# Moving the load buffer of a streaming decode kernel to a 256-byte boundary

## The chip, the cores and the metric

The kernel runs on one core of one Trainium2 chip. The metric is the device time of one execution in microseconds (us). Before the change it is 2518.53 us, the median of three runs.

## What is computed

One decode step of a layer that mixes attention with a gated MLP. The cache of keys and values is read once and used once, 32 heads of 65,536 positions of 128 numbers in bf16, so 1.07 GB of cache go through the core for a single output row of 512 numbers.

```python
def _A_ref(x, k_cache, v_cache, wq, wo):          # H=32, Sk=65536, Dh=128, Sq=1
    q = (x @ wq).reshape(B, Sq, H, Dh).transpose(0, 2, 1, 3)
    scores = einsum("bhqd,bhkd->bhqk", q, k_cache) * (Dh ** -0.5)
    o = einsum("bhqk,bhkd->bhqd", softmax(scores), v_cache)
    return o.transpose(0, 2, 1, 3).reshape(B, Sq, H * Dh) @ wo

def _B_ref(x, w_gate, w_up, w_down):              # D=512, F=1792
    return (silu(x @ w_gate) * (x @ w_up)) @ w_down

g = sigmoid((x * gate_w).sum(-1))
out = g * a + (1 - g) * b                         # a: attention, b: MLP
```

## The kernel before

One SBUF tensor, `mem` (L84), is 184 KB in each of the 128 partitions and takes every load from DRAM: the weights, the small vectors x and gate_w, all of K and V, and the output weights. Slots in it are counted in units of 1 KB (`KB = 512` bf16 numbers), and `at(kb, n)` (L109) gives the slice that starts at slot `kb`. K's halves go to slots 32 and 0, V's to 120 and 96 (`place`, L201), and weights use the same slots before and after K and V do.

A head is worked on in two halves (z = 0, 1) of 32,768 positions. One load brings one half of K or V of a head, 8 MB: each partition receives one contiguous row of 64 KB. Loads of that size are issued by SyncE from one queue (L224), in the order K half, V half, K half, V half, where V runs one head behind K. The loop over heads (L241 to L249) holds each load back until its slot is free: a K load waits until VectorE has transposed the half that lies there (`ktdone`), a V load until TensorE has multiplied it (`pvdone`).

VectorE turns K in pieces of 32 rows with 32x32 block transposes from `mem` into the small double buffer `kt` (L322, L415, L422). TensorE multiplies the pieces by the query (L472) into a bank of PSUM that holds a head's 65,536 scores as 128 x 512. VectorE and TensorE find the maximum (L336 to L338, L547, L549), ScalarE takes the exponential (L288), VectorE reorders the result into `pb` (L331), and TensorE multiplies it with V straight out of `mem`, 128 matmuls of 512 columns a head (L525). The order on each engine is written out by hand and held together by semaphores.

The start loads wq, w_gate, w_up and w_down (L213) and the first K half in two pieces (L228), and computes the query and the MLP. The end replaces the last V load by eight smaller ones with rows of 32 KB down to 1 KB (`tail`, L61 and L258), so that little work is left behind the last landing, and adds the output projection.

`sb` (L66) allocates an SBUF tensor with the allocator's default alignment. `mem` is the first tensor allocated in SBUF, and everything from `kt` on lies behind it.

Of the kernel before, what the change touches and what calls it, by code (L numbers as in the profile page):

```python
# [5 lines left out]
P = 128  # L6
KB = 512
# [5 lines left out]
BF16 = mybir.dt.bfloat16  # L13
# [8 lines left out]
def bass_gated_mix__mha_block_cached__swiglu_ffn__decode_kernel(  # L22
# [27 lines left out]
    MEM = 184  # L50
# [12 lines left out]
    WOJ, WO31 = V0, V0 + 1  # L63

    with ExitStack() as ctx:
        def sb(name, shape, dt):  # L66
            return ctx.enter_context(nc.sbuf_tensor(name, shape, dt))

        def psum(name, shape, dt):
            return ctx.enter_context(nc.psum_tensor(name, shape, dt))  # L70
# [10 lines left out]
        psW = psum("psW", [P, 512], F32)  # L81
        psZ = psum("psZ", [P, 512], F32)

        mem = sb("mem", [P, MEM * KB], BF16)  # L84
        kt = sb("kt", [P, 2, 2 * PR * 32], U32)
        qd = sb("qd", [P, H, 4, 4], BF16)
        qcur = sb("qcur", [P, 4, 4], BF16)
        pa = sb("pa", [P, 512], BF16)
# [542 lines left out]
```

## Time and profile before

| what | value |
|---|---|
| runs (median, lowest, highest) | 2518.53, 2518.48, 2519.13 us |
| span of the profiled execution, first to last instruction | 2517.0 us |
| busy: TensorE matmul, VectorE, ScalarE | 68%, 56%, 3% |
| bytes read from HBM, mean rate over the span | 1087.77 MB, 432 GB/s |
| mean granted TensorE clock | 0.721 |

The time of the profiled execution is its span, 2517.0 us; the median of the runs lies 1.5 us above it. In the profile, PE is TensorE, DVE is VectorE, ACT is ScalarE, SPq is SyncE's queue that issues DMAs, and L525 is line 525 of the kernel. A DMA is cut into packets, which the core's 16 DMA engines take. "Share of 16 engines" is the sum of the packets' durations over 16 times the length of the stretch that is looked at, so in a stretch shorter than a packet it can exceed 100%: a packet counts whole in the stretch in which it starts.

### The profile page before, as it was taken

The page shows a single profiled execution, that of the slowest core. Times are in us where ns is not written, and L with a number is a line of the kernel's source. Part 1 is how long each engine was busy: PE and PEld are TensorE (multiplying, and loading weights), DVE is VectorE, ACT ScalarE, POOL GpSimd, SP SyncE. Part 2 cuts the span into 40 slices and gives each one's busy share as a digit, 9 for nine tenths or more (in the row PEclk, how much of TensorE's full clock was granted, in tenths as well). Part 3 has the DMA queues.
Part 4 walks back from the last instruction along what each step waited for, and adds up shares of the span by engine and source line. Part 5 has one row for each costly group of instructions (what it writes and reads, how often), then busy time and mean ns, then how long its engine had stood idle before and what let it go on. Part 6 is the DMA issues. An engine that isn't in the chain of part 4 may idle for free.

```text
span 2517.0 us, 51694 instructions
## 1 busy us (share of the span) xinstructions
PE 1710.9 (68%) x21624; PEld 979.2 (39%) x21624; DVE 1411.7 (56%) x1683; ACT 64.6 (3%) x195; POOL 0.2 (0%) x4
## 2 busy tenths in 40 slices
PE   4667756667667677676776766766767767667677
PEld 3334433333433334333443333343334433334334
DVE  4764565554655645646456555465564564645653
ACT  0000000000000000000000000000000000000000
POOL 0000000000000000000000000000000000000000
PEclk8577767677677676776776767767767767677677
DMA  9999999999999999999999999999999999999999
GB/s 419 435 433 433 433 433 433 433 434 433 434 433 433 433 433 433 433 433 433 433 433 433 433 433 434 435 433 434 434 433 433 434 434 433 433 433 433 434 433 395
DMA packets 20471, 1087.93 MB, mean 432 GB/s; under 512 B 2283, under 2 KB 2669, under 8 KB 2925
## 3 DMA queue, kind: packets, MB, share of 16 engines
q1 hardware_dynamic: 20452, 1087.78, 99.9%
q8 instruction: 9, 0.15, 0.0%
q14 instruction: 2, 0.01, 0.0%
q10 hardware_dynamic: 8, 0.00, 0.0%
HBM read 1087.77 MB, written 0.00 MB: 432 GB/s over the span
## 4 chain that ended last, share of the span: by engine, by line
DMA 71%; PE 27%; DVE 1%; issue 1%; SPq 0%; ACT 0%; DVEq 0%
DMA mem<-in_A_v_cache_dram 68%; PE psO L525 27%; DMA mem<-in_A_k_cache_dram 2%; DVE kt L322 1%; DMA mem<-in_A_wq_dram 0%; DVE kt L415 0%; SPq L224 0%; PE psM L456 0%; DVE pb L331 0%; PE psS L472 0%; SPq L258 0%; PE psZ L600 0%; DVE sm L336 0%; PE psW L561 0%; PE psM L547 0%
## 5 line engine op out<-in xcount | busy, mean ns | idle before, releaser
L472 PE MATMUL psS<-qcur,kt 128*128 128x4 bf16 x16384 | 573.0, 169 | 728.7 <-DVE kt L415 413.2
L525 PE MATMUL psO<-mem,pb 128*4 128x512 bf16 x3968 | 1042.3, 429 | 34.5 <-DMA mem<-in_A_v_cache_dram 34.1
L472 PEld LDWEIGHTS psS<-qcur,kt 128*128 128x128 bf16 x16384 | 534.0, 105 | 792.1 <-issue 789.7
L422 DVE STREAM_TRANSPOSE kt<-mem 128x2048 uint32<-128x2048 uint32 x248 | 547.6, 2275 | 405.9 <-DMA mem<-in_A_k_cache_dram 405.9
L415 DVE STREAM_TRANSPOSE kt<-mem 128x2048 uint32<-128x2048 uint32 x248 | 551.3, 2280 | 239.3 <-DMA mem<-in_A_k_cache_dram 238.3
L525 PEld LDWEIGHTS psO<-mem,pb 128*4 128x4 bf16 x3968 | 359.8, 93 | 660.4 <-issue 241.3
L331 DVE COPY pb<-pa 32x64 bf16<-32x64 bf16 x1024 | 233.5, 228 | 15.1 <-ACT pa L288 1.5
L338 DVE TENSOR_REDUCE sc<-psM 1x1 f32<-1x128 f32 x32 | 8.9, 279 | 334.9 <-PE psM L547 334.9
L336 DVE TENSOR_REDUCE sm<-psS 128x1 f32<-128x512 f32 x32 | 22.1, 692 | 42.2 <-PE psS L472 42.2
L322 DVE STREAM_TRANSPOSE kt<-mem 128x2048 uint32<-128x2048 uint32 x16 | 35.4, 2277 | 16.9 <-DMA mem<-in_A_k_cache_dram 16.9
L286 ACT ACTIVATE sm<-psM 128x1 f32<-128x1 f32 x32 | 5.5, 171 | 1223.4 <-PE psM L549 1223.4
L282 ACT ACTIVATE oTn<-psT,gcol 128x1 f32 (+1 forms) x31 | 8.2, 264 | 1036.8 <-PE psT L499 1036.8
L499 PE MATMUL psT<-ident,orow 4*128 4x1 f32 x256 | 33.5, 248 | 0.5 <-ACT orow L280 0.5
L499 PEld LDWEIGHTS psT<-ident,orow 4*128 4x128 f32 x256 | 30.8, 186 | 1.2 <-ACT orow L280 0.6
L280 ACT ACTIVATE orow<-psO,sm 4x512 f32<-4x512 f32 x31 | 21.0, 678 | 130.3 <-PE psO L525 126.0
L288 ACT ACTIVATE pa<-psS,sm 128x512 bf16<-128x512 f32 x32 | 22.0, 687 | 1.0
L549 PE MATMUL psM<-sc,onesf 1*128 1x1 f32 x64 | 12.3, 259 | 11.9 <-DVE sc L338 11.9
L561 PE MATMUL psW<-pb,mem 128*128 128x1 bf16 x512 | 14.6, 165 | 6.5 <-DMA mem<-in_A_v_cache_dram 6.0
L549 PEld LDWEIGHTS psM<-sc,onesf 1*128 1x128 f32 x64 | 9.6, 186 | 21.5 <-DVE sc L338 21.5
L561 PEld LDWEIGHTS psW<-pb,mem 128*128 128x128 bf16 x512 | 14.1, 102 | 7.6 <-issue 5.5
L553 PEld LDWEIGHTS psM<-sm,onesf 128*128 128x128 f32 x64 | 9.7, 191 | 14.7 <-issue 13.5
L553 PE MATMUL psM<-sm,onesf 128*128 128x1 f32 x64 | 12.4, 264 | 1.1 <-ACT pa L288 1.1
(72 smaller groups left out, 93.1 us busy)
## 6 DMA issues: line engine op xcount, KB each, us to landing
mem<-in_A_v_cache_dram SPq DMA_DIRECT2D x3, 4096.0 KB, 29.4
mem<-in_A_k_cache_dram SPq DMA_DIRECT2D x2, 4096.0 KB, 38.9
mem<-in_A_wq_dram SPq DMA_DIRECT2D x1, 4096.0 KB, 12.3
mem<-in_A_wo_dram SPq DMA_DIRECT2D x1, 3968.0 KB, 36.6
mem<-in_A_v_cache_dram SPq DMA_DIRECT2D x1, 2048.0 KB, 32.9
mem<-in_B_w_gate_dram SPq DMA_DIRECT2D x1, 1792.0 KB, 16.1
mem<-in_B_w_up_dram SPq DMA_DIRECT2D x1, 1792.0 KB, 21.4
mem<-in_B_w_down_dram SPq DMA_DIRECT2D x1, 1792.0 KB, 25.2
```

The costliest lines, as they stand in the source:

```text
L288: nc.scalar.activation(pa[:], psS[:], ACT.Exp, bias=nbias, scale=SCALE, accum_out=rsum).then_inc(expdone, 1)
L322: nc.vector.transpose(kt[:, i % 2, :].rearrange("p (j r t) -> p r j t", j=2, t=32), src.rearrange("p (r j t) -> p r j t", j=2, t=32)).then ...
L331: last = nc.vector.tensor_copy(dst, sr)
L336: nc.vector.reduce_max(mxs, psS[:], AX_X).then_inc(s_mx, 1)
L415: nc.vector.transpose(kt[:, c % 2, :].rearrange("p (j r t) -> p r j t", j=2, t=32), src.rearrange("p (r j t) -> p r j t", j=2, t=32)).then ...
L422: nc.vector.transpose(kt[:, c % 2, :].rearrange("p (j r t) -> p r j t", j=2, t=32), src.rearrange("p (r j t) -> p r j t", j=2, t=32)).then ...
L472: last = nc.tensor.matmul(psS[:, o:o + 4] if j is None else psS[:, ds(j * (2 * PR) + o, 4)], ktb[b][:, je // 2, r, :, je % 2], qcur[:, je, ...
L499: last = nc.tensor.matmul(psT[:, 0:1], orow[0:4, i * Dh:(i + 1) * Dh], ident[0:4, i:i + 1], start=(i == 0), stop=(i == 3))
L525: last = nc.tensor.matmul(psO[0:4, :], pb[:, k_col[256 * z + r]:k_col[256 * z + r] + 4], vt[:, r * Dh:(r + 4) * Dh], start=(z == 0 and par ...
L549: nc.tensor.matmul(amx, onesf[0:1, :], gm, start=True, stop=True).then_inc(s_ar, 1)
L553: nc.tensor.matmul(Lt, onesf[:], rsum, start=True, stop=True).then_inc(s_L, 1)
L561: last = nc.tensor.matmul(psW[:, 0:1], vt[:, r * Dh:(r + 1) * Dh], pb[:, col:col + 1], start=(r0 + r == 0), stop=(r0 + r == R - 1))
```

## The change

`sb` gets an argument for the alignment, 32 bytes unless given, and `mem` is allocated with 256. In each partition `mem` then begins at byte 16640, which is 65 x 256, in place of byte 16512, which is 128 past 64 x 256. All slots of `mem` and every tensor behind it move up by 128 bytes. Nothing else changes: the instructions, their order, their waits and the DRAM sides of the loads are the same.

```diff
-        def sb(name, shape, dt):
-            return ctx.enter_context(nc.sbuf_tensor(name, shape, dt))
+        def sb(name, shape, dt, align=32):
+            return ctx.enter_context(nc.sbuf_tensor(name, shape, dt, align_bytes=align))
...
-        mem = sb("mem", [P, MEM * KB], BF16)
+        mem = sb("mem", [P, MEM * KB], BF16, 256)
```

## The prediction

> **What bounds the kernel now.** I read the page first for what is busy, then the chain of waits for what the end hangs on, then the DMA queue's own waits for how early each load is issued, and last the DMA packets in short stretches for what one packet costs.
>
> ```profile
> span 2517.0 us, 51694 instructions
> PE 1710.9 (68%) x21624; PEld 979.2 (39%) x21624; DVE 1411.7 (56%) x1683; ACT 64.6 (3%) x195; POOL 0.2 (0%) x4
> DMA  9999999999999999999999999999999999999999
> GB/s 419 435 433 433 433 433 433 433 434 433 434 433 433 433 433 433 433 433 433 433 433 433 433 433 434 435 433 434 434 433 433 434 434 433 433 433 433 434 433 395
> DMA packets 20471, 1087.93 MB, mean 432 GB/s; under 512 B 2283, under 2 KB 2669, under 8 KB 2925
> q1 hardware_dynamic: 20452, 1087.78, 99.9%
> DMA 71%; PE 27%; DVE 1%; issue 1%; SPq 0%; ACT 0%; DVEq 0%
> ```
>
> The DMA engines are busy in every slice, at 433 GB/s from the third slice to the next to last, while TensorE and VectorE are idle for a third and for nearly half of the span. The chain gives 27% to PE, which looks like a second limit. It is not one, and three pieces of the chain show why:
>
> ```profile
> 143.60 10.69 PE psO L525 x40
> ...
> 1006.82 26.85 DMA mem<-in_A_v_cache_dram
> 1033.71 11.07 PE psO L525 x40
> ...
> 2465.67 10.19 PE psO L525 x40
> ```
>
> From the first of these PE pieces to the last there are 60 steps, each of one 8 MB load of K and one of V. That is (2465.67 - 143.60) / 60 = 38.701 us a step, and 19.351 us a load. The load issued at 1006.82 lands 26.85 us later: it spends 7.5 us behind the load ahead of it and 19.35 us moving. The chain follows the issue through PE because a V buffer comes free only when PE has read it, but the queue never runs dry. What sets the time is therefore how fast the 16 engines swallow packets. Per packet the trace says this (one pitch of a load; then short stretches with one kind of packet in them):
>
> ```profile
> DMA packets 144, 8.39 MB, mean 434 GB/s; under 512 B 16, under 2 KB 16, under 8 KB 16
> ...
> q1 hardware_dynamic: 144, 8.39, 100.2%
> ```
>
> This is the stretch 985.00 to 1004.35 us. Each engine handles 9 packets: 8 rows of 64 KB and a completion packet under 512 B. Their durations add up to 1.002 x 19,350 = 19,389 ns, 38 more than the pitch of 19,351, so a packet overlaps its neighbour by about 4.2 ns. I take that off every duration below.
>
> ```profile
> DMA packets 2, 0.00 MB, mean 1 GB/s; under 512 B 2, under 2 KB 2, under 8 KB 2
> ...
> q1 hardware_dynamic: 2, 0.00, 11.2%
> ```
>
> ```profile
> DMA packets 14, 0.01 MB, mean 239 GB/s; under 512 B 0, under 2 KB 14, under 8 KB 14
> ...
> q1 hardware_dynamic: 14, 0.01, 67.1%
> ```
>
> ```profile
> DMA packets 7, 0.10 MB, mean 502 GB/s; under 512 B 0, under 2 KB 0, under 8 KB 0
> ...
> q1 hardware_dynamic: 7, 0.10, 117.0%
> ```
>
> The first is 315.51 to 315.52 us, two completion packets: 0.112 x 160 / 2 = 9.0 ns each. The second is 2513.42 to 2513.48, fourteen 1 KB rows: 0.671 x 960 / 14 = 46.0 ns. The third is 14.10 to 14.30, seven 14 KB rows (14,336 B) of the MLP weights: 1.170 x 3200 / 7 = 534.9 ns. From the second to the third are 13,312 B and 488.9 ns, so an engine moves 27.23 B per ns once a row runs. A 1 KB row is then 37.6 ns of bytes. Its 46.0 less the overlap of 4.2 is 41.8, so it pays **4.2 ns beyond its bytes**. A 64 KB row is (19,389 - 9) / 8 = 2422.5 ns, less 4.2, which is 2418.3; its bytes are 2406.8, so it pays 11.5 beyond them. That last figure is soft: one ns in the 488.9 shifts it by 5. A completion packet pays 9.0 - 4.2 - 0.1 = 4.7 ns beyond its few bytes.
>
> **The change part by part.** It removes and adds no instruction. It moves the base of mem from 128 past a multiple of 256 bytes to such a multiple. Every slot of mem is a multiple of 1 KB, so every row of every load moves from the middle of a 256-byte block to its start. Everything allocated after mem moves up by 128 bytes.
>
> *The rows.* All packets but those under 512 B are rows, and nearly all of them are in q1, the queue of the loads into mem: (20,471 - 2,283) / 16 = 1137 rows on each engine. Since the engines are busy to the end, a ns saved on a row is 1137 ns off the span. No row of the trace starts on a boundary, so the saving is not shown and I bound it. Below: a row may pay nothing for its start, and then nothing is saved. Above: the whole surplus may come from the start, 11.5 ns on each of the 64 KB rows, of which there are
>
> ```profile
> mem<-in_A_k_cache_dram SPq DMA_DIRECT2D x63, 29.5
> mem<-in_A_v_cache_dram SPq DMA_DIRECT2D x62, 27.5
> ```
>
> 125 x 8 = 1000 on an engine, and 4.2 ns on the other 137: 11.5 + 0.6 = 12.1 us. Below nothing I treat as a rival. Between the ends I take the time of half a block: a row that starts in the middle of a block has to touch one block more than its bytes fill, and the unused half is 128 / 27.23 = 4.7 ns. The nearest row is the 1 KB row with its 4.2 ns, short of that by half a ns. The sum is 1137 x 4.7 = 5.3 us.
>
> The Trainium skill bears on this in "DMA: Bandwidth & Descriptors", section "How a descriptor splits into AXI transactions": a transaction has to start at a 256-byte boundary, and a descriptor that does not start there pays beats for the unused bytes in front. It says so of reading, and mem is the written side here; the 4.2 ns of the trace agree in size, but show no start on a boundary to set against them. By its figures half a block is 4 beats at 850 MHz, an estimate of 4.7 ns, which would make the same sum.
>
> *The engines that read mem.* TensorE's reads in the value matmuls and VectorE's transposes get a new base too:
>
> ```profile
> L525 PE MATMUL psO<-mem,pb 128*4 128x512 bf16 x3968 | 1042.3, 429 | 34.5 <-DMA mem<-in_A_v_cache_dram 34.1
> L422 DVE STREAM_TRANSPOSE kt<-mem 128x2048 uint32<-128x2048 uint32 x248 | 547.6, 2275 | 405.9 <-DMA mem<-in_A_k_cache_dram 405.9
> L415 DVE STREAM_TRANSPOSE kt<-mem 128x2048 uint32<-128x2048 uint32 x248 | 551.3, 2280 | 239.3 <-DMA mem<-in_A_k_cache_dram 238.3
> ```
>
> I cost these at nothing, either way. VectorE waits 644 us for K, and a V load waits 7.5 us behind another, so PE would have to become 7.5 us slower in a step, on about 17 us of value matmuls (1042.3 / 62), before the queue ran dry. A gain there would go into the same waits. With that cover gone, each us a step would cost 60 us.
>
> *The faster queue.* At 2 x 8 x 4.7 ns the step shrinks by 0.075 us, and the wait behind the other load by a like amount out of 7.5. What is late next is still the DMA queue.
>
> *The end.* From the last row on nothing changes: the final matmuls, the copy and the store hang on the last landing, which comes earlier by the whole sum.
>
> The sum against the profiled execution is 2517.0 - 5.3 = 2511.7 us of span. The median of the runs, 2518.53, lies 1.5 above that span, so the forecast is 2518.5 - 5.3 = **2513.2 us**.
>
> **The rivals.**
>
> *A. A fixed price of any packet: no change.* The completion packet writes no row of mem and yet pays 4.7 ns, about what the 1 KB row pays. If that is the price of starting any packet, it stays, and the time is 2518.5 us. For it: the equal sums, from the same trace. Against it: a completion is another kind of write, with a start of its own that the trace does not show, so the two 4 to 5 ns need not have one cause. The skill's same page, section "Why small descriptors are slow (HBM only)", has a rule that speaks against the change in this way: about 3 cycles on each packet whatever its start. An estimate at the page's 850 MHz is 3.5 ns of the 4.2, which would leave 0.7 ns a row, under 1 us in all. No run here tells the two rules apart. That the base does not move as stated comes out as this rival too.
>
> *B. The whole surplus goes.* If being off the boundary also makes the long rows stumble (a row that sits astride each block all the way), all of the 11.5 ns goes: 2518.5 - 12.1 = 2506.4 us. For it: a 64 KB row pays more than a 1 KB row. Against it: the figure is soft, and 64 KB rows land while the engines read mem, which the 14 KB rows hardly do.
>
> *C. Slower: writes fall into step with the engines' reads.* A 64 KB row pays 11.5 - 4.2 = 7.3 ns more than a short one. If that comes from meeting the reads of L525, L415 and L422, and a row on a boundary meets them more often, because the reads then start on the same boundary, a doubling adds 7.3 ns to each of 1000 rows: 2518.5 + 7.3 = 2525.8 us. It decides from 5.0 ns a row on, where the loss passes 0.2%. Against it: the rate in the page's slices is the same 433 or 434 nearly everywhere, and writes and reads that met by chance would make it wander.
>
> **How the numbers follow.** About 0.2%, here 5.0 us, is what a measurement of this kernel can tell from no change; the three runs shown lie within 0.65 us. The forecast's 5.3 us is barely past that, and 4.2 ns a row instead of 4.7 would be 4.8 us and short of it. Chances: forecast 0.42 (0.27 past the bound, 0.15 short of it), A 0.29, B with everything between 6 and 12 us 0.17, C 0.12. Faster by over 0.2% is 0.27 + 0.17 = 0.44, within it 0.15 + 0.29 = 0.44, slower 0.12. The forecast's own range is 2512.4 to 2514.2 (5.4 ns to 3.8 ns a row). The range to hold 8 in 10 takes in A with a us of spread, and B to its end, leaving out C: 2506.4 to 2519.5.
>
> **What would show it.** If the forecast is right, the step of the chain falls from 38.701 to about 38.626 us, the 1 KB rows near the end take about 42 ns in place of 46.0, the completion packets stay at 9.0, and the slices read 434 GB/s. With A the step stays within 0.01 us and the 1 KB rows stay at 46. With B the step is near 38.52 and the slices read 435 or 436. With C the short rows gain or stay, and the 64 KB rows grow past 2427 ns. TensorE's and VectorE's durations of L525, L415 and L422 should be as before in every case. If they are not, and the DMA queue has gaps, the argument from packets was the wrong one.

## The result, and the profile after

The changed kernel takes 2513.86 us (median of 18 runs, 2513.69 to 2514.11) against 2518.36 for the kernel before (18 runs, 2518.17 to 2519.13). That is 4.50 us less, a ratio of 0.9982 with a 95% interval of 0.9976 to 0.9988. The forecast was 2513.2, so the saving was put at 5.3 and is 4.5. It falls just short of the 0.2% that the prediction used as its bound.

From the page of the changed kernel, the span, the rate in slices and the packets:

```profile
span 2512.4 us, 51694 instructions
...
GB/s 420 436 434 434 434 435 434 434 434 434 434 434 434 434 434 434 434 434 434 434 434 434 434 434 434 434 434 434 434 434 434 434 434 434 435 434 434 434 435 402
DMA packets 20470, 1087.93 MB, mean 433 GB/s; under 512 B 2282, under 2 KB 2668, under 8 KB 2924
```

The slices went from 433 to 434 GB/s, with as many packets but one. From its chain of waits, the two pieces that answer to those at 143.60 and 2465.67 before (start, length, what):

```profile
142.99 10.33 PE psO L525 x40
...
2461.26 11.70 PE psO L525 x40
```

Sixty steps take 2318.27 us, 38.638 each, where they took 38.701. So 3.80 us of the gain lie in the steady loop, 0.61 in the start and 0.19 in the end (51.14 us from the last of these pieces on, before 51.33); together 4.6 of span. The loop is 960 rows of 64 KB on each engine: 3.80 / 960 = **4.0 ns a row**.

The engines that read mem, from the changed kernel's page:

```profile
L525 PE MATMUL psO<-mem,pb 128*4 128x512 bf16 x3968 | 1040.6, 428 | 32.9 <-DMA mem<-in_A_v_cache_dram 32.6
L422 DVE STREAM_TRANSPOSE kt<-mem 128x2048 uint32<-128x2048 uint32 x248 | 547.6, 2275 | 402.3 <-DMA mem<-in_A_k_cache_dram 402.3
L415 DVE STREAM_TRANSPOSE kt<-mem 128x2048 uint32<-128x2048 uint32 x248 | 551.3, 2280 | 240.3 <-DMA mem<-in_A_k_cache_dram 239.3
```

Means of 428, 2275 and 2280 ns are those of before, within 1 ns. Now the packets, in the stretch 990.0 to 992.4 us, the kernel before first, then the changed one:

```profile
DMA packets 16, 1.05 MB, mean 437 GB/s; under 512 B 0, under 2 KB 0, under 8 KB 0
...
q1 hardware_dynamic: 16, 1.05, 100.9%
```

```profile
DMA packets 27, 1.05 MB, mean 437 GB/s; under 512 B 11, under 2 KB 11, under 8 KB 11
...
q1 hardware_dynamic: 27, 1.05, 101.0%
```

Both hold sixteen 64 KB rows, the second also 11 completion packets of 9 ns. Before: 1.009 x 38,400 / 16 = 2421.6 ns a row. After: (1.010 x 38,400 - 99) / 16 = 2417.8. The long rows lost about 4 ns. (A tenth of a percent is 2.4 ns a row here.) The records of the single packets in the two traces are finer: from 200 to 2300 us the 64 KB rows take anything from 2418 to 2433 ns before, 2421.7 on average, and exactly 2418 after. The expectations below call the first a spread, or stumbling.

Now 1 KB rows near the end of the changed kernel, 2509.00 to 2509.06 us:

```profile
DMA packets 15, 0.01 MB, mean 222 GB/s; under 512 B 2, under 2 KB 15, under 8 KB 15
...
q1 hardware_dynamic: 15, 0.01, 64.2%
```

Less two completion packets of 9 ns: (0.642 x 960 - 18) / 13 = **46.0 ns, as in the stretch before**. The forecast said 42. Over all 384 of them the records give 46.9 before and 46.0 after. So at most 0.9 of the 4.2 ns that a 1 KB row pays beyond its bytes was the price of its start there, and the amount came out nearly right from the wrong row. The experiments ask where the 4 ns of a long row came from.

### The profile page after: what moved, and what is told of

The parts are those of the page before. It is cut to its first block, busy times and chain, and to the rows that moved or that the text cites. A ratio compares the mean times of both kernels' runs of the same rounds, so it can differ in the third digit from the quotient of the medians.

```text
span 2512.4 us, 51694 instructions
## 1 busy us (share of the span) xinstructions
PE 1709.8 (68%) x21624; PEld 978.8 (39%) x21624; DVE 1411.8 (56%) x1683; ACT 64.6 (3%) x195; POOL 0.2 (0%) x4
## 4 chain that ended last, share of the span: by engine, by line
DMA 70%; PE 27%; DVE 1%; issue 1%; SPq 0%; ACT 0%; DVEq 0%
DMA mem<-in_A_v_cache_dram 67%; PE psO L525 27%; DMA mem<-in_A_k_cache_dram 2%; DMA mem<-in_A_wo_dram 1%; DVE kt L322 1%; DMA mem<-in_A_wq_dram 0%; DVE kt L415 0%; SPq L224 0%; PE psM L456 0%; DVE pb L331 0%; PE psS L472 0%; PE psM L547 0%; DVE sm L336 0%; PE psZ L600 0%; PE psM L549 0%
## 5 line engine op out<-in xcount | busy, mean ns | idle before, releaser
L525 PE MATMUL psO<-mem,pb 128*4 128x512 bf16 x3968 | 1040.6, 428 | 32.9 <-DMA mem<-in_A_v_cache_dram 32.6
L422 DVE STREAM_TRANSPOSE kt<-mem 128x2048 uint32<-128x2048 uint32 x248 | 547.6, 2275 | 402.3 <-DMA mem<-in_A_k_cache_dram 402.3
L415 DVE STREAM_TRANSPOSE kt<-mem 128x2048 uint32<-128x2048 uint32 x248 | 551.3, 2280 | 240.3 <-DMA mem<-in_A_k_cache_dram 239.3
L525 PEld LDWEIGHTS psO<-mem,pb 128*4 128x4 bf16 x3968 | 359.4, 93 | 657.5 <-issue 238.4
```

The lines of the kernel that those rows point to most:

```text
L415: nc.vector.transpose(kt[:, c % 2, :].rearrange("p (j r t) -> p r j t", j=2, t=32), src.rearrange("p (r j t) -> p r j t", j=2, t=32)).then ...
L422: nc.vector.transpose(kt[:, c % 2, :].rearrange("p (j r t) -> p r j t", j=2, t=32), src.rearrange("p (r j t) -> p r j t", j=2, t=32)).then ...
L525: last = nc.tensor.matmul(psO[0:4, :], pb[:, k_col[256 * z + r]:k_col[256 * z + r] + 4], vt[:, r * Dh:(r + 4) * Dh], start=(z == 0 and par ...
```

## The experiments

Theory 1, formed on the two traces: a row of mem that does not start on a 256-byte block loses time as it is written, on the DMA path alone. Rival 2: such writes meet the engines' reads and writes of SBUF. Rival 3: mem has no part, and one of the tensors behind it gained.

### Which tensor, and does the place of the cut matter?

Three kernels are whole; only places in SBUF differ.

```diff
 # e1_rest_moved: mem stays at 16512, the tensors behind it move up by 128
         mem = sb("mem", [P, MEM * KB], BF16)
+        sb("gap", [P, 64], BF16)
```

> mem stays at 16512, everything behind it moves up by 128 bytes as in the changed kernel. Theory 1 (the rows of mem astride 256-byte blocks stumble): as before, 2518.4 us, step 38.70 us, 64 KB rows spread over 2418 to 2426 ns. Rival 3 (it was one of the tensors behind mem that gained): 2513.9 us, step 38.64 us, 64 KB rows at 2418 ns.

```diff
 # e11_mem_only: mem at 16640, the tensors behind it as far into a block as before
+        sb("gap", [P, 64], BF16)
         mem = sb("mem", [P, MEM * KB], BF16)
+        sb("gap2", [P, 64], BF16)
```

> The whole kernel with mem at 16640 as in the changed one, and 128 bytes left free behind mem too, so that the tensors behind it keep their places within a 256-byte block as before the change. If mem alone matters: 2513.9 us, step 38.64 us, 64 KB rows 2418 ns. If the place of the others has a part: between 2513.9 and 2518.4.

```diff
 # e2_base_64: mem at 16576, 192 past a block
+        sb("gap", [P, 32], BF16)
         mem = sb("mem", [P, MEM * KB], BF16)
```

> mem at 16576, a multiple of 64 but not of 128 or 256 (192 past a block). Theory 1: a row astride blocks stumbles wherever it cuts them, so 2518.4 us give or take 1, and 64 KB rows spread over some ns. If the place of the cut matters (a 64-byte piece is dearer or cheaper than a 128-byte one), the mean row is off 2422 ns and the time with it by 1 us a ns. If only 64-byte boundaries counted, 2513.9 us. The forecast's mechanism, one block touched in excess per row at 4.7 ns, would give 46 ns for a 1 KB row here and less in the changed kernel, which the changed kernel has already denied.

The same two pieces of the chain in each (the added lines make L525 into L526 or L527), first e1, then e11, then e2:

```profile
143.64 10.14 PE psO L526 x40
...
2465.77 11.30 PE psO L526 x40
```

```profile
143.04 10.70 PE psO L527 x40
...
2461.29 10.39 PE psO L527 x40
```

```profile
143.44 10.99 PE psO L526 x40
...
2465.57 10.45 PE psO L526 x40
```

| run | mem at | median us | ratio to before, interval | step us |
|---|---|---|---|---|
| e1 | 16512 | 2518.41 | 1.000 (0.9991 to 1.001) | 38.702 |
| e11 | 16640 | 2513.83 | 0.9982 (0.9972 to 0.9991) | 38.638 |
| e2 | 16576 | 2518.74 | 1.0001 (0.9992 to 1.0011) | 38.702 |

The whole gain is that of mem, and none that of the tensors behind it. (That mem lies at 16512 and 16640 is the allocator's figure and stands in no trace. The runs agree with it: 128 more bytes ahead of mem, in e11, do what the alignment to 256 does.) At 192 bytes past a block the loss is that of 128, within 0.33 us. If a row paid for the unused bytes in front of it, 64 more bytes at 27.2 B per ns would be 2.4 ns on 1137 rows, 2.7 us more.

### Do the engines' reads play a part?

Two kernels hold the loads alone: the 64 halves of K and the first 62 of V, in rows of 64 KB, alternating between two slots. The query, the transposes, all matmuls, the softmax and the weights are left out, and the output is zeros.

```diff
 # e3_quiet_128; e4_quiet_256 has a gap of 128 bytes ahead of mem
+            for n, (kind, h, z) in enumerate(seq):
+                if n >= 2:
+                    sp.wait_ge(d[n % 2], 16 * (n // 2))
...
+                sp.dma_start(mem[:, kb * KB:kb * KB + HR * Dh], src).then_inc(d[n % 2], 16)
```

> The loads alone: 64 K and 62 V half heads of 64 KB rows into two slots of mem at 16512, each held back until the load before in its slot has landed; no query, no transposes, no matmuls, no weights, and zeros for an output. Theory 1 (the stumbling lies on the DMA path alone): 64 KB rows spread over 2418 to 2426 ns, pitch of a load 19.35 us, span about 126 x 19.35 = 2438 us and a few us. Rival 2 (writes astride blocks meet the engines' reads and writes of SBUF): with the engines idle every 64 KB row takes 2418 ns as in the changed kernel, pitch 19.32 us, span 4 us shorter and equal to the next run's.

> The same loads alone with mem at 16640. Theory 1: every 64 KB row 2418 ns, pitch 19.32 us, span 4 us below the run at 16512. Rival 2: the same rows and pitch, but no difference from the run at 16512.

From two runs each, the medians are 2444.86 us (2444.64 to 2445.07) at 16512 and 2440.65 (2440.61 to 2440.70) at 16640: 4.21 us apart, on 126 x 8 = 1008 rows an engine, 4.2 ns a row. The gain of the whole kernel stands there with TensorE, VectorE and ScalarE idle, so rival 2 falls, and with it the ground of the prediction's rival C. The cost is on the path of the DMA alone.

### The side that is read, or the side that is written?

```diff
 # e5_both_128 (mem at 16512) and e6_source_128 (mem at 16640)
-    SHIFT = 0
+    SHIFT = 64
...
                 lo = lo + SHIFT if 2 * h + z < 2 * H - 1 else lo
```

> The loads alone with mem at 16512, and the DRAM side of every load but the last of K and of V also moved by 128 bytes, so that rows start 128 past a block on both sides (the data is the cache's, shifted by 64 numbers). Theory 1a (what hurts is that a block read in DRAM falls on two blocks of mem): both sides cut alike, so 64 KB rows take one fixed time again, near 2418 ns or up to 4.7 more, and the pitch does not wander. Theory 1b (only the written side's start counts): rows spread over 2418 to 2426 ns as at 16512 before, span 2443.7 us.

> The loads alone with mem at 16640 and only the DRAM side moved by 128 bytes. Theory 1a: the sides are cut unlike, so rows spread over 2418 to 2426 ns and the span is that of mem at 16512, 2443.7 us. Theory 1b: rows at 2418 ns, 2439.2 us. A price of the read's start, half a block of 4.7 ns a row, would show as a constant 2422 to 2423 ns and 2444 us.

The line of the loads' queue in the stretch 1200.00 to 1296.72 us, five loads long, for e3, e4, e5 and e6 in this order (720 packets in each, of which 80 are completions):

```profile
q1 hardware_dynamic: 720, 41.94, 100.2%
```

```profile
q1 hardware_dynamic: 720, 41.94, 100.0%
```

```profile
q1 hardware_dynamic: 720, 41.94, 100.2%
```

```profile
q1 hardware_dynamic: 720, 41.94, 100.0%
```

The last column is the whole reading: 0.2% of 96.72 us on 40 rows is 4.8 ns a row, give or take 2.4 from rounding. It follows the base of mem (e3 and e5 at 16512, e4 and e6 at 16640) and not the DRAM side (moved in e5 and e6). The packet records, from 200 to 2300 us again, have rows of 2421.7 ns on average in e3 and in e5, 2418.3 in e4 and 2418.0 in e6. The medians of two runs say the same: 2444.86, 2440.65, 2445.10 (2444.50 to 2445.71) and 2441.01 (2440.36 to 2441.67). Theory 1b holds: **only the start of the written side counts**.

This is where the Trainium skill and the runs part. "DMA: Bandwidth & Descriptors", section "How a descriptor splits into AXI transactions", charges a read that starts off a 256-byte block for the bytes in front. Where the caches start in DRAM is in no trace; at a multiple of 128 bytes, either e4 or e6 reads off a block, and neither pays for it: 2440.65 and 2441.01 us. And the written side, for which that section states no price, pays the same at 128 as at 192 past.

### Finer cuts

```diff
 # e7_base_32, from e3: 160 past a block; e8_base_16 has 8 in place of 16: 144 past
-                sp.dma_start(mem[:, kb * KB:kb * KB + HR * Dh], src).then_inc(d[n % 2], 16)
+                sp.dma_start(mem[:, kb * KB + 16:kb * KB + 16 + HR * Dh], src).then_inc(d[n % 2], 16)
```

> The loads alone, written 32 bytes further than 16512 (160 past a block, a multiple of 32 and not of 64). If every start off a 256-byte block is alike, as 64 and 128 were: mean 64 KB row near 2422 ns, span 2443.7 us. If the finer cut is dearer, the mean row grows, by 1 us of span for each ns.

> The loads alone, written 16 bytes further than 16512 (144 past a block, a multiple of 16 and not of 32). If starts off a block are alike, 2443.7 us; if a piece of 16 bytes at each block's edge costs a step of its own, one in 8 or 9 of the time, 2700 us and more.

2444.62 and 2445.02 us, against 2444.86 at 16512: no cut is dearer than another within 0.3 us. Among starts 128 to 192 bytes past a block the place makes no difference. Starts less than 128 past were not run.

### By the row or by the byte?

That the 1 KB rows hardly moved from 46.0 ns spoke against a price by the row, and for long rows that lose a little with every block. Rows of 16 KB decide it: the same bytes in four times as many rows.

```diff
 # e9_rows16_128 (16512); e10_rows16_256 (16640): loads of 2 MB, eight slots of 16 KB
...
-                sp.dma_start(mem[:, kb * KB:kb * KB + HR * Dh], src).then_inc(d[n % 2], 16)
+                sp.dma_start(mem[:, kb * KB:kb * KB + n2 // P], src).then_inc(d[n % ND], 16)
```

> The loads alone at 16512 in rows of 16 KB: the same bytes in 504 loads of 2 MB, eight slots. Fixed costs add about 16 us to the span of the 64 KB rows at either base (3024 more rows on an engine at 4.7 ns, 378 more completion packets at 5.9), so 2455 us at 16640. If a start off the boundary costs by the byte: about 1 ns a row, 2459.5 us. If by the row, 4.1 ns on 4032 rows: 2472 us.

> The same with mem at 16640: 2455 us, rows at 611 ns throughout. The distance to the run at 16512 is 4 to 5 us if the cost goes by the byte, 16 us if by the row.

2475.60 us (2475.46 to 2475.73) and 2459.05 (2458.86 to 2459.23): 16.55 us on 4032 rows, **4.1 ns a row**. That is the price of a 64 KB row with a quarter of the bytes, so it goes by the row. (The spans, 2474.4 and 2457.5 us, are both some 2.5 above what was expected by the row; why was not looked into.) Three short stretches show when it is paid: e9 at 12.0 to 12.6 us, e9 at 1000.0 to 1000.6, and e10 at 1000.0 to 1000.6:

```profile
DMA packets 18, 0.25 MB, mean 410 GB/s; under 512 B 3, under 2 KB 3, under 8 KB 3
...
q1 hardware_dynamic: 18, 0.25, 95.8%
```

```profile
DMA packets 15, 0.25 MB, mean 410 GB/s; under 512 B 0, under 2 KB 0, under 8 KB 0
...
q1 hardware_dynamic: 15, 0.25, 96.2%
```

```profile
DMA packets 17, 0.26 MB, mean 437 GB/s; under 512 B 1, under 2 KB 1, under 8 KB 1
...
q1 hardware_dynamic: 17, 0.26, 101.9%
```

Less the completions, a 16 KB row takes (0.958 x 9600 - 27) / 15 = 611.3 ns early in e9, 0.962 x 9600 / 15 = 615.7 later, and (1.019 x 9600 - 9) / 16 = 610.8 in e10. The rows off the boundary are not charged at first, and are later. In the packet records of e9 the charge sets in at about 25 us, when each engine has taken some 38 rows; in e10 it does not. The 14 KB rows of the prediction are rows 9 to 32 of each engine, in the first 26 us of the kernel, and take 535 ns at the median both before and after the change; so they looked clean though they started off a block.

### Rows of 4 KB

```diff
 # e12_rows4_128, from e3: each 64 KB row in 16 rows of 4 KB, 4352 bytes apart in mem
-        slots = (32, 96)
+        slots = (0, 96)
...
-                sp.dma_start(mem[:, kb * KB:kb * KB + HR * Dh], src).then_inc(d[n % 2], 16)
+                dst = mem[:, kb * KB:kb * KB + 16 * 2176].rearrange("p (a f) -> p a f", f=2176)[:, :, 0:2048]
+                sp.dma_start(dst, src.rearrange("p (a f) -> p a f", a=16)).then_inc(d[n % 2], 16)
```

> The loads alone at 16512, each 64 KB row cut into 16 rows of 4 KB that lie 4352 bytes apart in mem (17 blocks of 256, so each starts 128 past a block); 16,128 rows on an engine. In the changed kernel's end a 4 KB row follows the next after 155.3 ns. If a start off the boundary costs 4.1 ns a row at this size too, as at 64 and 16 KB: 159.4 ns a row, span 16,128 x 159.4 = 2571 us and some 5 for the ends. If short rows are charged less, as the 1 to 4 KB rows at the end of the kernel before suggest (1 to 3 ns): 2525 to 2560 us. Free: 2510 us.

From its page, the span and the packets:

```profile
span 2585.5 us, 157 instructions
...
DMA packets 260073, 1056.98 MB, mean 409 GB/s; under 512 B 2024, under 2 KB 2024, under 8 KB 260072
```

(260,073 - 2,024) / 16 = 16,128 rows an engine. The 64 KB loads of e4 leave 2439.2 - 126 x 19.319 = 5.0 us for the ends, and 126 completions at some 6 ns are 0.8. So a row takes (2585.5 - 5.8) / 16,128 = 159.95 ns. For a 4 KB row on the boundary there are those at the end of the changed kernel (2505.30 to 2505.35 us):

```profile
DMA packets 2, 0.01 MB, mean 164 GB/s; under 512 B 0, under 2 KB 0, under 8 KB 2
...
q1 hardware_dynamic: 2, 0.01, 39.8%
```

0.398 x 800 / 2 = 159.2 ns, less an overlap of 4.2 (the prediction's) to 3.6 (the same sum for the changed kernel: (8 x 2417.8 + 9 - 19,319) / 9), is 155.0 to 155.6. The difference is 4.4 to 4.9 ns a row, above the 4.1 expected (the span was to be some 2576 us and is 9.5 more), so short rows are not let off in a steady stream, and on 4 KB rows the loss is 3%. In the packet records all 128 rows of 4 KB of the changed kernel have 159 ns, and each starts 155.3 after the one before, which makes the difference 4.7. No run of 4 KB rows on the boundary in bulk was made, so this rests on those few, which lie one to a partition and not sixteen.

## Why the prediction was right, and where it was not

*What bounds the kernel.* Right. The DMA queue set the time, nothing came to stand behind it, and the step fell to 38.638 us where 38.626 was forecast.

*A saving by the row, on every row, about half a block.* Right in kind: e9 and e10 show a price by the row, e3 and e4 that no engine has a part in it, e5 and e6 that it is the written side's start. Off in size: 4.0 ns on the long rows for 4.7, so 1000 rows gave 4.0 us where the forecast had 4.7. The other 137 rows were to give 0.6; what is left of the measured 4.50 is 0.5. They are not all alike: the end, with 86 of the rows, gained only 0.19 us. The packet records show it: the change took 4.1 ns off the 32 KB rows there, 1.8 to 3.3 off those of 3 to 16 KB, 0.9 off those of 1 KB. The start gained 0.61, more than its 89 rows at 4 ns (0.36). What the rest is was not looked into; part may be chance, since e2, off the boundary too, has its first piece at 143.44, 0.16 earlier than the kernel before.

*The row that it was taken from.* Wrong, and this is the step that failed. The prediction took the 4.2 ns that a 1 KB row pays beyond its bytes as the nearest row to the price. Those 4.2 are still there on the boundary, as rival A had it: a price that a packet pays wherever it starts, and the completion packet pays about as much. The price of the start was in the other figure, the 11.5 ns of the 64 KB row, which the prediction called soft. Between 1 KB and 64 KB rows on the boundary the engine now moves 64,512 B in 2417.8 - 46.0 ns, 27.20 B per ns. Rows of 4 KB lie on the same line: 46.0 + 3072 / 27.20 = 158.9 ns, and 159.2 was read. So on the boundary long and short rows pay the same 4 to 5 ns beyond their bytes. Against that slope the long rows before paid 8 to 9 (2418.3 - 65,536 / 27.20 = 8.9; the prediction's slope of 27.23, from rows that were not charged, was nearly right, and its 11.5 too large): two prices of nearly equal size, and the prediction matched its sum to the wrong one. That the forecast came within 0.7 us is in part luck.

*Half a block of unused bytes.* The size was near, the picture is not shown. Starts 128, 144, 160 and 192 past a block cost the same, so between these the price does not grow with the bytes in front. What these starts have in common is that each row touches one block more than it fills; that this is what costs the time was not tested.

*The rivals.* A was right about the short rows and wrong about the whole. B's stumbling at each block is a price by the byte, which e9 and e10 do not show. C is ruled out by the result, and e3 and e4 leave the engines' reads no part in the gain. The prediction gave 0.15 to its own mechanism ending short of 0.2%; that is the case that came.

## What to carry to other kernels

Where the DMA engines set the time, put the base of a buffer that takes loads, and the distance between its rows, on a multiple of 256 bytes. Off it, by 128 to 192 bytes, each row of a steady stream cost 4 to 5 ns here: next to nothing in rows of 64 KB (0.17%), about 3% in rows of 4 KB. To size such a thing, compare long and short packets in the steady part of a trace: a surplus that the completion packets pay too is likely a fixed price that no address will remove.

## What the runs showed that was not expected

The price does not appear at once, and what counts seems to be rows and not time. In e9 the 16 KB rows took 611.3 ns at 12 us, as if they lay on a boundary, and 615.7 at 1000 us. In e12, from 6 to 7 us,

```profile
q1 hardware_dynamic: 101, 0.41, 100.4%
```

a 4 KB row took 1.004 x 16,000 / 101 = 159.1 ns, as on a boundary too. In the packet records the charge sets in at 8 to 9 us there and at about 25 us in e9: in both after some 38 rows of each engine, though the rows of one hold four times the bytes of the other's. From then on the 4 KB rows of one engine repeat a pattern of four, such as 159, 161, 164 and 171 ns. In the kernel before, most of the 1 KB rows at the very end were free (46.0 ns in the stretch that the prediction shows, 46.9 on average). It looks as if something took up the excess for a while. What that is, and why the steady price is 4.0 to 4.2 ns at 64 and 16 KB but nearer 4.7 at 4 KB, stays open.
